# One fused adaLN / multi-query attention / SwiGLU block: from a generator that interleaves by budget to a list-scheduled task graph, with wider exps, denominators summed on VectorE and the MLP as filler

## The chip, the cores and the metric

The kernel runs on one core of one Trainium2 chip. The metric is the device time of one execution in microseconds (us). "Fast runs" are those of the undisturbed state; only these are compared. The engines are PE (TensorE, matrix multiply), ACT (ScalarE, exp and tanh), DVE (VectorE), POOL (GpSimd) and SP (issues DMA). The profile gives the share of the full TensorE clock that was granted; "warm" below means about 1.0, "cold" about 0.5. PV is the product of the exponentials with the values, and the *slot* of a group of matmuls is the time from its start on PE to the start of the next group.

## The reference

```python
# x: 2048 x 1024, 32 query heads of 32, ONE key and value head of 32, F = 3584
sa, ca, ga, sb, cb, gb = split(silu(c) @ w_mod)              # six modulation vectors of 1024
h = layernorm(x) * (1 + ca) + sa
q, k, v = h @ wq, h @ wk, h @ wv                             # k and v are shared by all heads
x = x + ga * (softmax(q k^T / sqrt(32)) v) @ wo
h = layernorm(x) * (1 + cb) + sb
x = x + gb * ((silu(h @ w1) * (h @ w3)) @ w2)
```

The work is cut into 4 blocks of 512 queries. A block has 8 "heads" (each a group of 4 query heads, packed into the 128 rows of the array), and a head has 16 key tiles of 128 keys. One key tile needs four score matmuls, 4 x 512 columns of exp, four PV matmuls and, in some form, the softmax denominators. There are 512 key tiles in all. The MLP of a block can only start when the attention of that block is done, so it runs as *filler* for PE beside the attention of the next block, and the MLP of the last block runs alone.

## The kernel before

All matmul filler comes from one queue of generators. After each key tile the queue is drained until a budget of 1700 ns is spent, in pieces of up to eight matmuls. The order of the instructions on PE is fixed by this, without regard to what waits for what.

```python
def exp_pair(kt, pair):                       # two exps of 1024 columns per key tile
    T.emit("act", lambda e: e.activation(U[:, uslot, g0:g0 + 2, :], S4[:, g0:g0 + 2, :], ACT.Exp, scale=SCALE), ...)
...
for kt in range(NKT):
    exp_pair(kt, 0)
    exp_pair(kt, 1)
    if kt + 1 < NKT:
        for g in range(4): s_mm(kt + 1, g)    # next scores, into the same four banks
    for g in range(4): pv(kt, g)              # PV sums, one bank
    for g in range(4): dd(kt, g)              # denominators: ones x U, another bank
    ...
    yield "B"                                 # -> drain(BUDGET)
...
BUDGET = 1700.0
MM512 = 216.0
CH = 8
def drain(budget):
    spent = 0.0
    while posts and spent < budget:
        spent += step(posts[0])               # one piece of filler, up to CH matmuls
```

PSUM has eight banks: four for scores, one for PV, one for denominators, two for all filler.

The softmax here doesn't subtract the row's maximum and nothing guards it: scores larger than these inputs give would overflow.

## Time and profile before

| | before |
|---|---|
| median of 4 runs | 1787.5 us (1779.3 to 1788.8) |
| first exp | 126.6 us |
| end of block 0 | 460.8 us |
| blocks 1, 2, 3 | 369.3, 367.1, 371.7 us |
| from there to the end | 209.8 us |

The block ends are read from the timeline: each head ends with one copy of the PV sums out of PSUM, and the eighth copy of a block is its end.

The head of the profile page of the kernel before; each figure is busy time and share of the span, the digits are tenths in 40 equal slices, PEclk the granted clock.

```profile
PE 1525.3 (86%) x9792; PEld 478.9 (27%) x9920; DVE 542.7 (31%) x844; ACT 1111.0 (62%) x1248; POOL 45.5 (3%) x76
...
PE   2476899989979999888899999887999988968997
...
ACT  2913578888667775687677755886677657821100
...
PEclk7687995555779999955899999557899997568999
```

No engine is full throughout. The clock row shows the pattern: it falls to 5 in four places, and these are the places where ACT is at 7 to 8 and the filler has run out.

Stretches of the kernel before: the stretch, its length, busy us (instructions) of PE, PE weight loads, DVE, ACT and POOL, then granted clock, DMA share and GB/s.

```profile
1249.00:1493.00 244.00, 226.03 (x1609) 78.88 (x1640) 83.23 (x139) 163.69 (x183) 0.00 (x0) 0.98 0.36 87
1493.00:1563.00 70.00, 63.50 (x394) 11.09 (x386) 10.54 (x6) 60.99 (x66) 0.00 (x0) 0.52 0.13 32
1600.00:1778.00 178.00, 157.85 (x722) 67.81 (x734) 65.53 (x137) 16.72 (x28) 0.00 (x0) 0.96 0.49 119
```

The first is block 3 with filler: PE is 93% busy at full clock and ACT 67%. In the second the filler is used up: ACT 87%, clock 0.52. The third is the MLP of the last block: PE is 89% busy and no other engine more than 37%.

The timeline of one filled key tile in the kernel before (start, length, engine, line, operation, output and inputs, count, idle time before):

```profile
557.12 0.40 PE L675 MATMUL S<-QT,KT 32*128 32x512 bf16 x4
...
557.45 0.40 PE L699 MATMUL AD<-HT,V 128*32 128x512 bf16 x4
...
557.58 1.94 ACT L689 ACTIVATE HT<-S 128x1024 bf16<-128x1024 f32 x2 [0.63 <-PE S L675]
557.67 0.39 PE L708 MATMUL AD<-HT,ONES 128*32 128x512 bf16 x4
557.99 1.90 PE L845 MATMUL PB<-HT,W1S 128*128 128x512 bf16 x8
...
559.83 0.40 PE L675 MATMUL S<-QT,KT 32*128 32x512 bf16 x4
```

Read the starts, not the lengths (ends of matmuls are modelled): scores 0.33, PV 0.22, denominators 0.32, eight filler matmuls 1.84, together 2.71 us, in which ACT works 1.94. ACT waits for PE.

The costliest groups before (line, engine, operation, shapes, count | busy us, mean ns | idle before):

```profile
L689 ACT ACTIVATE HT<-S 128x1024 bf16<-128x1024 f32 x1024 | 979.3, 1023 | 302.0 <-PE S L675 301.8
L675 PE MATMUL S<-QT,KT 32*128 32x512 bf16 x2048 | 353.8, 477 | 88.4 <-ACT HT L689 87.9
L708 PE MATMUL AD<-HT,ONES 128*32 128x512 bf16 x2048 | 261.7, 490 | 0.0
```

### The profile page before, as it was taken

The page shows a single profiled execution, that of the slowest core. Times are in us where ns is not written, and L with a number is a line of the kernel's source. Part 1 is how long each engine was busy: PE and PEld are TensorE (multiplying, and loading weights), DVE is VectorE, ACT ScalarE, POOL GpSimd, SP SyncE. Part 2 cuts the span into 40 slices and gives each one's busy share as a digit, 9 for nine tenths or more (in the row PEclk, how much of TensorE's full clock was granted, in tenths as well). Part 3 has the DMA queues.
Part 4 walks back from the last instruction along what each step waited for, and adds up shares of the span by engine and source line. Part 5 has one row for each costly group of instructions (what it writes and reads, how often), then busy time and mean ns, then how long its engine had stood idle before and what let it go on. Part 6 is the DMA issues. An engine that isn't in the chain of part 4 may idle for free.

```text
span 1778.8 us, 23745 instructions
## 1 busy us (share of the span) xinstructions
PE 1525.3 (86%) x9792; PEld 478.9 (27%) x9920; DVE 542.7 (31%) x844; ACT 1111.0 (62%) x1248; POOL 45.5 (3%) x76
## 2 busy tenths in 40 slices
PE   2476899989979999888899999887999988968997
PEld 0231321111223333311233333112333332123433
DVE  0530331121254441221543422114344321144431
ACT  2913578888667775687677755886677657821100
POOL 2300400000000000000000000000000000000000
PEclk7687995555779999955899999557899997568999
DMA  8104100000003343310033524200233443003465
GB/s 292 33 33 154 37 1 1 1 1 1 1 25 95 96 113 71 82 44 1 12 91 97 127 52 76 71 1 1 72 95 95 87 84 91 1 0 95 142 131 106
DMA packets 249373, 115.97 MB, mean 65 GB/s; under 512 B 119472, under 2 KB 242352, under 8 KB 249264
## 3 DMA queue, kind: packets, MB, share of 16 engines
q1 hardware_dynamic: 247344, 107.10, 24.0%
q0 software_dynamic: 1920, 7.34, 1.2%
q8 instruction: 78, 1.28, 0.3%
q14 instruction: 31, 0.25, 0.1%
HBM read 110.23 MB, written 4.19 MB: 64 GB/s over the span
## 4 chain that ended last, share of the span: by engine, by line
PE 74%; ACT 11%; DVE 9%; issue 4%; DMA 2%; POOL 0%; DVEq 0%; ACTq 0%; POOLq 0%; SPq 0%
PE S L675 13%; PE AD L699 12%; PE PB L861 11%; PE PB L845 11%; PE PB L850 10%; ACT HT L689 8%; PE AD L708 6%; PE PB L768 4%; PE PB L644 3%; DVE ADSB L738 2%; DVE O2B L867 1%; PE PB L477 1%; DVE ST L516 1%; ACT HT L596 1%; DVE ADSB L736 1%
## 5 line engine op out<-in xcount | busy, mean ns | idle before, releaser
L689 ACT ACTIVATE HT<-S 128x1024 bf16<-128x1024 f32 x1024 | 979.3, 1023 | 302.0 <-PE S L675 301.8
L675 PE MATMUL S<-QT,KT 32*128 32x512 bf16 x2048 | 353.8, 477 | 88.4 <-ACT HT L689 87.9
L699 PE MATMUL AD<-HT,V 128*32 128x512 bf16 x2048 | 261.1, 486 | 1.3 <-ACT HT L689 1.2
L708 PE MATMUL AD<-HT,ONES 128*32 128x512 bf16 x2048 | 261.7, 490 | 0.0
L845 PE MATMUL PB<-HT,W1S 128*128 128x512 bf16 x861 | 210.3, 385 | 27.2 <-DVE TT L831 16.3
L850 PE MATMUL PB<-HT,W3S 128*128 128x512 bf16 x865 | 207.5, 380 | 3.9 <-DVE TS L829 1.9
L861 PE MATMUL PB<-HHT,W2S 128*128 128x512 bf16 x861 | 206.5, 380 | 3.9 <-issue 2.3
L675 PEld LDWEIGHTS S<-QT,KT 32*128 32x128 bf16 x2048 | 75.1, 94 | 468.1 <-ACT HT L689 425.0
L827 ACT ACTIVATE TS<-PB 128x512 bf16<-128x512 f32 x112 | 66.9, 597 | 184.9 <-PE PB L845 184.9
L736 DVE COPY ADSB<-AD 128x1024 f32<-128x1024 f32 x32 | 39.1, 1221 | 389.4 <-PE AD L708 389.4
L845 PEld LDWEIGHTS PB<-HT,W1S 128*128 128x128 bf16 x896 | 80.1, 99 | 150.4 <-issue 40.6
L850 PEld LDWEIGHTS PB<-HT,W3S 128*128 128x128 bf16 x896 | 81.4, 98 | 120.4 <-issue 33.4
L861 PEld LDWEIGHTS PB<-HHT,W2S 128*128 128x128 bf16 x896 | 80.5, 98 | 113.7 <-issue 31.7
L738 DVE RECIPROCAL ADSB<-ADSB 128x512 f32<-128x512 f32 x32 | 107.3, 3353 | 1.1
L829 DVE TENSOR_SCALAR TS<-TS 128x512 bf16<-128x512 bf16 x112 | 32.8, 293 | 233.6 <-ACT TS L827 233.6
L699 PEld LDWEIGHTS AD<-HT,V 128*32 128x32 bf16 x2048 | 56.0, 96 | 177.8 <-issue 152.9
L833 DVE TENSOR_TENSOR HHT<-TT,PB 128x512 bf16<-128x512 bf16 x112 | 76.9, 687 | 88.1 <-PE PB L850 85.1
L867 DVE TENSOR_SCALAR O2B<-PB,GBT 128x512 bf16<-128x512 f32 x32 | 24.0, 751 | 223.9 <-PE PB L861 223.9
L831 DVE TENSOR_TENSOR TT<-TS,PB 128x512 bf16<-128x512 bf16 x112 | 77.1, 688 | 3.8
L768 PE MATMUL PB<-WO,ATT 128*128 128x512 bf16 x245 | 63.9, 412 | 11.9 <-DVE ATT L740 10.9
L708 PEld LDWEIGHTS AD<-HT,ONES 128*32 128x32 bf16 x2048 | 57.7, 103 | 0.0
L644 PE MATMUL PB<-HT,HHT 128*128 128x512 bf16 x216 | 52.7, 388 | 2.9 <-DVE QT L652 1.4
(84 smaller groups left out, 520.1 us busy)
## 6 DMA issues: line engine op xcount, KB each, us to landing
W1S<-in_B_w_dram SPq DMA_DIRECT2D x56, 512.0 KB, 3.9
W3S<-in_B_w_dram SPq DMA_DIRECT2D x56, 512.0 KB, 4.3
W2S<-in_B_w_dram SPq DMA_DIRECT2D x32, 896.0 KB, 6.0
X<-in_A_x_dram SPq DMA_DIRECT2D x4, 1024.0 KB, 13.2
W1S<-in_w_mod_dram SPq DMA_DIRECT2D x4, 1024.0 KB, 5.1
W3S<-in_w_mod_dram SPq DMA_DIRECT2D x4, 1024.0 KB, 5.1
out_dram<-X SPq DMA_DIRECT2D x4, 1024.0 KB, 5.4
W1S<-in_w_mod_dram POOLq DMA_DIRECT2D x3, 1024.0 KB, 10.1
```

Of the source, the lines that this page charges most:

```text
L644: fns = [lambda e, cc=cc, f=f, ap=ap: e.matmul(ap, WQ[:, cc, f * P:(f + 1) * P], HT[:, cc, qb * 512:(qb + 1) * 512], start=(cc == 0), stop ...
L675: T.emit("pe", lambda e, kt=kt, g=g: e.matmul(S4[:, g, :], KT[32 * g:32 * (g + 1), kt * P:(kt + 1) * P], QT[32 * g:32 * (g + 1), f, qb * 5 ...
L689: T.emit("act", lambda e, uslot=uslot, g0=g0: e.activation(U[:, uslot, g0:g0 + 2, :], S4[:, g0:g0 + 2, :], ACT.Exp, scale=SCALE), reads=[( ...
L699: T.emit("pe", lambda e, kt=kt, g=g, uslot=uslot, first=first, last=last: e.matmul(APS[32 * g:32 * (g + 1), :], V[:, kt, :], U[:, uslot, g ...
L708: T.emit("pe", lambda e, kt=kt, g=g, uslot=uslot, first=first, last=last: e.matmul(DPS[32 * g:32 * (g + 1), :], ONES[:], U[:, uslot, g, :] ...
L738: T.emit("dve", lambda e: e.reciprocal(ADSB[:, 1, :], ADSB[:, 1, :]), reads=["ADSB1"], writes=["ADSB1"])
L768: fns = [lambda e, f=f, tti=tti, fb=fb, pbk=pbk: e.matmul(PB[pbk][:, :], ATT[:, f, tti * P:(tti + 1) * P], WO[:, f, fb * 512:(fb + 1) * 51 ...
L831: T.emit("dve", lambda e, gs=gs: e.tensor_tensor(TT1[:, gs, :], TS[:, gs, :], PB0[:, :], ALU.mult), reads=[("TS", gs), ("PB", 0)], writes= ...
L833: T.emit("dve", lambda e, gs=gs, ft=ft: e.tensor_tensor(HHT[:, ft, :], TT1[:, gs, :], PB1[:, :], ALU.mult), reads=[("TT1", gs), ("PB", 1)] ...
L845: fns = [lambda e, cc=cc, slot=slot, sub=sub, H2T=H2T: e.matmul(PB0[:, :], W1S[:, slot, cc, sub * P:(sub + 1) * P], H2T[:, cc, :], start=( ...
L850: fns = [lambda e, cc=cc, slot=slot, sub=sub, H2T=H2T: e.matmul(PB1[:, :], W3S[:, slot, cc, sub * P:(sub + 1) * P], H2T[:, cc, :], start=( ...
L861: fns = [lambda e, fc=fc, slot=slot: e.matmul(PB0[:, :], W2S[:, slot, fc, :], HHT[:, fc, :], start=(fc == 0), stop=(fc == NF - 1)) for fc ...
```

## The change

The intent: describe all instructions as a graph of tasks with assumed durations, simulate the engines, and emit each engine's instructions in the order in which the simulation started them. Scores go first, then PV, then denominators, then filler, one matmul at a time, and a filler group gets a PSUM bank only when the simulation has one free. With it come a new cut of the exps, denominators that are mostly summed on VectorE, attention that starts as soon as the first 512 keys exist, and layernorms without passes for shift and scale. The core of the diff (almost every line of the file changes):

```diff
+            pick = min((c for c in cands if c[0] <= t + (slack if c[1].prio <= 1 else 0.001)), key=key)
+                    if n.cls == "S": r = 0                       # scores first
+                    elif n.cls == "V": ...  r = 1 or 4           # PV
+                    elif n.cls == "D": r = 2                     # denominators
+                    else: r = 3                                  # filler
...
-    S4 = psb("S4", [P, 4, 512], F32)
-    AD = psb("AD", [P, 2, 512], F32)
+    S5 = nc.alloc_psum_tensor("S5", [P, 5, 512], F32)            # banks 0-2, and 3 or 4 in turn
+    A = nc.alloc_psum_tensor("A", [P, 512], F32)
...
-    U[:, uslot, g0:g0 + 2, :], S4[:, g0:g0 + 2, :], ACT.Exp      # twice per key tile
+    U[:, u, 0:3, :], S5[:, 0:3, :], ACT.Exp                      # 1536 columns
+    U[:, u, 3, :], S5[:, s1, :], ACT.Exp                         # 512 columns, s1 = 3 + i % 2
...
-    DPS[32 * g:32 * (g + 1), :], ONES[:], U[:, uslot, g, :]      # for every key tile
+    TR[:, tr, :], TR[:, tr, :], U[:, u]..., ALU.add              # three adds of 2048 columns per four key tiles
+    PB[g.bank][...], ONES[:], TR[:, tr, ...]                     # ones-matmuls on the four sums of a head
...
+    # layernorm: (1 + scale) and shift applied per partition while the transposes leave PSUM
+    dst(c), PBH[g.bank][...], MODC[:, fm, c:c + 1], MODC[:, fs, c:c + 1], ALU.mult, ALU.add
...
+    g = grp()                                                    # filler: one task per matmul
+    for i0 in range(0, n, per): ...                              # per = 1
```

## The prediction

> **What bounds the kernel now.** No single engine does. The page gives PE 86%, ACT 62%, DVE 31% busy; the stretch table splits the 1778.8 us. Head: the first exps come at 126.6 us, then one pair per 6.8 us until 181, behind modulation blocks. Filled attention (516-756, 882-1127, 1249-1493): granted clock 0.98-1.00, PE about 93% busy, ACT about 67%. In the timeline one key tile takes 2.70 us there: scores 0.33, PV 0.22, denominators 0.32, eight MLP matmuls 1.83; two exps cover 1.94, so ACT waits for PE. Unfilled attention (210-463, 756-830, 1127-1197, 1493-1563): clock 0.50-0.60 and 2.09 us a key tile (4.18 for two); PE has no MLP work left. The Trainium skill, "TensorE: Matmul & The Clock Gate", Part 1, says that an array that is not busy enough runs at half clock; this trace agrees (0.50 against 1.00). Tail: last exp at 1567.8, then 211 us of WO, layernorm and MLP, PE-bound.
> So blocks alternate between too much filler and none.
>
> **What changes.**
> - Denominators: 2048 matmuls (262 us of PE busy) become 512; about 0.25 us a key tile leaves PE. VectorE gains 384 adds of 128x2048 bf16. A 128x1024 bf16 add takes 692 ns now; I estimate 1.22 us each, 470 us in all, so DVE goes from 543 to about 950 us busy.
> - Exps: 1024 at 1023 ns become 512 of 1536 columns plus 512 of 512. From 1023 (1024 columns) and 597 (512 columns) I estimate 1450 + 597: no ACT gain. The gain meant is that the next scores fit under the small exp. But banks 0-2 stay single: exp 1.45, then release plus scores plus visibility, about 0.1 + 0.46 us warm (score start 557.12, exp start 557.58) or 0.1 + 0.68 cold (321.78 to 322.46). That is a chain of about 2.0 us warm, 2.2 cold, a key tile.
> - Head: modulation as columns, the shift and scale folded into the transposes' evacuation, attention started per 512 keys: first exp near 45 us.
> - MLP spread matmul by matmul over the blocks; two PSUM banks for all filler.
> - Scale and shift passes of both layernorms (692 ns each), sqrt and its table loads go.
>
> **The sum.** PE per key tile warm: scores 0.33, PV 0.27, denominators 0.06, switches 0.1; filler of a block (672 MLP + 64 WO matmuls at about 0.22, transposes) about 165 us / 128 = 1.29. Together 2.05, level with the 2.0 us chain, so neither hides the other: I take 2.2-2.3.
> Head 45; block 0 (little filler, cold clock, layernorms of three blocks inside) 310; blocks 1-3, 290 each, 870; tail 205. Sum 1430 us. Nearly all PE saving is on the critical path; the rest comes from head and filler balance.
>
> **Right or wrong shows in:** first exp before 60 us; exps spaced about 2.2 us in all blocks, ACT busy 75% or more; clock near 1.0 in blocks 1-3, near 0.5-0.6 in block 0; denominator matmuls near 65 us; DVE 60-70% busy; last exp near 1225 us, then a tail near 200.
>
> **What would make it wrong.** DVE in order at about 80% in blocks 1-3: PSUM evacuations queued behind 1.2 us adds would stall filler, thus scores (slower, up to 1520). A static order built from assumed durations could stall PE's queue. Half clock in filled blocks would cost 200 us. Better interleaving could bring 1340.
>
> Predicted 1430 us, 1350 to 1520; faster 0.97, within 2% 0.02, slower 0.01.

## The result, and the profile after

| | before | after |
|---|---|---|
| median | 1787.5 us | 1398.9 us (1398.3 to 1400.4, 4 runs) |
| first exp | 126.6 us | 31.7 us |
| end of block 0 | 460.8 us | 338.4 us |
| blocks 1, 2, 3 | 369.3, 367.1, 371.7 us | 287.6, 287.7, 286.2 us |
| from there to the end | 209.8 us | 196.5 us |

The ratio is 0.7845 (95% interval 0.7823 to 0.7867). All ratios here are the mean time of one kernel's fast runs over that of the other's of the same rounds, so not quite the ratio of the medians. Of the 382 us between the two spans, 122 lie in the head and block 0, 247 in blocks 1 to 3 and 13 in the tail.

The head of the page after:

```profile
PE 1209.6 (87%) x8689; PEld 424.9 (30%) x8689; DVE 939.8 (67%) x1174; ACT 1046.8 (75%) x1142; POOL 17.3 (1%) x34
...
PE   4498985555899999988899999978999999789997
...
ACT  2378998888889999888899998989999989311100
...
PEclk9597995555899999998999999979999999889999
```

Apart from slice 2, in the head, the clock now has one hole, in slices 7 to 10, where before it had four.

Stretches after (columns as before):

```profile
200.00:338.00 138.00, 72.26 (x552) 12.36 (x544) 76.89 (x75) 119.91 (x125) 0.00 (x0) 0.53 0.12 29
414.00:560.00 146.00, 145.53 (x1047) 49.55 (x1046) 110.14 (x129) 133.80 (x153) 0.00 (x0) 1.00 0.37 100
883.00:913.00 30.00, 25.34 (x199) 8.27 (x197) 20.62 (x24) 28.29 (x31) 0.00 (x0) 0.96 0.57 125
```

These are three regimes of one loop. In the first there is no filler: PE is half idle and cold, and a head takes 36.1 us. In the second PE is busy 145.5 of 146 us, and a head takes 36.6 us. In the third, the last head of a block, PE is warm and nearly but not quite full, and a head takes 30.6 us. The same head time of 36 us has two opposite causes in the first two.

The timeline after, in a filled stretch:

```profile
453.12 0.40 PE L606 MATMUL S<-QT,KT 32*128 32x512 bf16 x4
...
453.45 1.25 PE L703 MATMUL PB<-QT,WREG 128*128 128x512 bf16 x5
453.56 1.45 ACT L613 ACTIVATE UREG<-S 128x1536 bf16<-128x1536 f32 x1
...
454.54 0.81 PE L711 MATMUL PB<-QT,WREG 128*128 128x512 bf16 x3
454.91 0.59 ACT L706 ACTIVATE HREG<-PB 128x512 bf16<-128x512 f32 x1
...
455.28 0.40 PE L606 MATMUL S<-QT,KT 32*128 32x512 bf16 x4
455.39 0.60 ACT L615 ACTIVATE UREG<-S 128x512 bf16<-128x512 f32 x1
```

Eight filler matmuls and one score group now fit into 2.16 us. (PV is done for two key tiles at once: its eight matmuls follow in the next key tile, which takes 2.27 us with six of filler.) The next scores no longer wait for the second exp: they start at 455.28, before the 512-column exp at 455.39.

The timeline after, in the cold stretch:

```profile
283.02 0.59 ACT L615 ACTIVATE UREG<-S 128x512 bf16<-128x512 f32 x1
283.18 0.61 PE L606 MATMUL S<-QT,KT 32*128 32x512 bf16 x4 [1.56 <-ACT UREG L613]
...
283.84 1.45 ACT L613 ACTIVATE UREG<-S 128x1536 bf16<-128x1536 f32 x1 [0.23 <-PE S L606]
```

PE had been idle for 1.56 us and could start the scores only when the wide exp had released banks 0 to 2. The next wide exp starts 0.66 us after the scores, and that is 0.23 us later than ACT could have taken it. This is a chain, not a full engine.

The groups that answer to those of before:

```profile
L613 ACT ACTIVATE UREG<-S 128x1536 bf16<-128x1536 f32 x512 | 744.1, 1453 | 150.7 <-PE S L606 140.1
L646 DVE TENSOR_TENSOR UREG<-UREG 128x2048 bf16<-128x2048 bf16 x256 | 310.9, 1214 | 82.8 <-ACT UREG L615 82.4
L606 PE MATMUL S<-QT,KT 32*128 32x512 bf16 x2048 | 222.5, 425 | 121.5 <-ACT UREG L613 118.3
L615 ACT ACTIVATE UREG<-S 128x512 bf16<-128x512 f32 x512 | 305.7, 597 | 0.0
...
L658 PE MATMUL PB<-UREG,ONES 128*32 128x512 bf16 x512 | 41.0, 449 | 1.7 <-DVE UREG L646 1.7
```

The exps cost what they cost before: 1453 + 597 ns against 2 x 1023. Per column this is (1453 - 597) / 1024 = 0.84 ns, which agrees with the 1.2 GHz that the Trainium skill gives in "ScalarE: Activation LUTs", Specifications. The adds take 1214 ns; the Trainium skill, "VectorE: DVE Perf Modes", "The perf-mode tier table", has 1224 ns for a bf16 add of 2048 elements, and this trace agrees. The denominator matmuls fall from 261.7 to 41.0 us busy.

### The profile page after: what moved, and what is told of

It is laid out like the page before. It is cut to its first block, busy times and chain, and to the rows that moved or that the text cites. A ratio compares the mean times of both kernels' runs of the same rounds, so it can differ in the third digit from the quotient of the medians.

```text
span 1396.4 us, 21161 instructions
## 1 busy us (share of the span) xinstructions
PE 1209.6 (87%) x8689; PEld 424.9 (30%) x8689; DVE 939.8 (67%) x1174; ACT 1046.8 (75%) x1142; POOL 17.3 (1%) x34
## 4 chain that ended last, share of the span: by engine, by line
PE 77%; ACT 11%; DVE 7%; issue 3%; POOL 1%; DMA 0%; SPq 0%; DVEq 0%; POOLq 0%; ACTq 0%
PE PB L703 15%; PE PB L711 15%; PE PB L722 14%; PE S L606 13%; ACT UREG L613 9%; PE A L624 7%; PE PB L682 4%; PE PB L506 4%; PE PB L658 3%; DVE ST L421 2%; DVE UREG L646 2%; ACT UREG L615 1%; DVE XN L438 1%; PE PB L452 1%; PE PB L490 1%
## 5 line engine op out<-in xcount | busy, mean ns | idle before, releaser
L613 ACT ACTIVATE UREG<-S 128x1536 bf16<-128x1536 f32 x512 | 744.1, 1453 | 150.7 <-PE S L606 140.1
L646 DVE TENSOR_TENSOR UREG<-UREG 128x2048 bf16<-128x2048 bf16 x256 | 310.9, 1214 | 82.8 <-ACT UREG L615 82.4
L606 PE MATMUL S<-QT,KT 32*128 32x512 bf16 x2048 | 222.5, 425 | 121.5 <-ACT UREG L613 118.3
L615 ACT ACTIVATE UREG<-S 128x512 bf16<-128x512 f32 x512 | 305.7, 597 | 0.0
L703 PE MATMUL PB<-QT,WREG 128*128 128x512 bf16 x896 | 226.6, 386 | 1.3 <-DVE QT L467 1.3
L640 DVE TENSOR_TENSOR UREG<-UREG 128x2048 bf16<-128x2048 bf16 x128 | 155.6, 1215 | 106.3 <-ACT UREG L615 105.7
L711 PE MATMUL PB<-QT,WREG 128*128 128x512 bf16 x896 | 222.6, 381 | 0.0
L722 PE MATMUL PB<-HREG,WREG 128*128 128x512 bf16 x896 | 214.3, 380 | 0.0
L624 PE MATMUL A<-UREG,V 128*32 128x512 bf16 x2048 | 178.3, 429 | 6.5 <-ACT UREG L615 5.6
L667 DVE RECIPROCAL DSB<-DSB 128x128 f32<-128x128 f32 x128 | 116.7, 932 | 0.9
L703 PEld LDWEIGHTS PB<-QT,WREG 128*128 128x128 bf16 x896 | 80.1, 98 | 118.8 <-issue 43.0
L711 PEld LDWEIGHTS PB<-QT,WREG 128*128 128x128 bf16 x896 | 81.0, 98 | 111.9 <-issue 29.0
L722 PEld LDWEIGHTS PB<-HREG,WREG 128*128 128x128 bf16 x896 | 79.2, 98 | 108.0 <-issue 30.3
L506 PE MATMUL PB<-HREG,WREG 128*128 128x512 bf16 x256 | 63.9, 385 | 0.1
```

What stands on the lines that cost most here:

```text
L506: g = mm_group(NC, lambda e, b, c: e.matmul(b[:], WQ[:, c, f * P:(f + 1) * P], HT[:, c, sl], start=c == 0, stop=c == NC - 1), lambda c: [( ...
L606: r = e.matmul(S5[:, b, j * qn:(j + 1) * qn], KT[32 * gg:32 * gg + 32, kt * P:(kt + 1) * P], QT[32 * gg:32 * gg + 32, f, q0:q0 + qn], star ...
L613: G.add("act", lambda e, u=u: e.activation(U[:, u, 0:3, :], S5[:, 0:3, :], ACT.Exp, scale=SCALE), reads=["S3"], writes=[("U", u, 0)] + uk, ...
L615: G.add("act", lambda e, u=u, s1=s1: e.activation(U[:, u, 3, :], S5[:, s1, :], ACT.Exp, scale=SCALE), reads=[("S1", s1)], writes=[("U", u, ...
L624: r = e.matmul(A[32 * gg:32 * gg + 32, 0:qn], V[:, kt, :], U[:, pu, gg, j * qn:(j + 1) * qn], start=kt == 0, stop=kt == NT - 1, tile_posit ...
L640: G.add("dve", lambda e, tr=tr, u=u, fu=first_u: e.tensor_tensor(TR[:, tr, :], U[:, fu].rearrange("p g s -> p (g s)"), U[:, u].rearrange(" ...
```

## The experiments

The theory after the result: in blocks 1 to 3 PE is full and its work sets the time; in block 0 the chain exp, scores, exp sets it, lengthened by the cold clock; and the gain comes from less PE work, an earlier start and filler that is spread well. The rivals: VectorE's in-order queue sets the pace of the filler; the cut of the exps is the main source; the spread alone is.

### half_adds: is VectorE the bound?

```diff
-  TR[:, tr, :], TR[:, tr, :], U[:, u]..., ALU.add
+  TR[:, tr, 0:1024], TR[:, tr, 0:1024], U[:, u]...[:, 0:1024], ALU.add     # and the ones-matmuls read only these columns
```

> The changed kernel with each of the 384 adds cut to 1024 of its 2048 columns (wrong denominators on purpose), static order unchanged. VectorE falls from 940 to about 730 us busy. Theory (PE and the score-exp chain bound): within 1%, 1385 to 1400 us. Rival (VectorE's queue bounds the filled blocks): faster by 40 us or more, filled heads from 36.6 to 34 us or less.

Measured: 1386.0 us (ratio 0.7766 against 0.7845 for the full change; the result is wrong). Taking some 200 us off VectorE's 940 gave 1%. The stretch from 414 to 560 us in this kernel:

```profile
414.00:560.00 146.00, 144.90 (x1036) 49.41 (x1034) 86.20 (x130) 134.26 (x152) 0.00 (x0) 1.00 0.36 98
```

VectorE fell from 110 to 86 us there, and PE stayed full with the same number of matmuls. The filled heads stay at 36.6 us. VectorE is not the bound of the filled blocks. The 13 us are gained in small pieces: 4 us in block 0 and 1 to 3 us in each of the first two heads of blocks 1 and 2, where layernorm work stands in VectorE's queue.

### exp1024 and den_on_pe, and both again

These undo the cut of the exps, and on top of it the sums on VectorE.

```diff
 # exp1024: two score groups of two matmuls, two exps of 1024 columns, four banks
+ for hf in range(2):
+     scores of heads 2*hf, 2*hf+1 -> S5[:, 2*hf:2*hf+2, :]
+     exp U[:, u, 2*hf:2*hf+2, :] <- S5[:, 2*hf:2*hf+2, :], prio=0
 # den_on_pe: as exp1024, and ones x U for every key tile into the free bank S5[:, 4, :]; no adds
 # exp1024_b, den_on_pe_b: the same two, the second exp with prio=hf (0, then 1)
```

> The changed kernel with the exps cut as before: two of 1024 columns, and the scores as two groups of two matmuls, four banks. Theory (filled blocks are PE-bound, the exp cut gives ACT nothing): filled heads stay at 36.6 us for 16 key tiles or gain up to 1.6 us from one more switch of PE per key tile; the cold heads of block 0 fall from 36.1 towards 31 us, because the next scores of one pair run under the exp of the other. Total 1375 to 1440 us. Rival (the wide exp with its five banks is a main source of the gain): 1460 us or more, blocks 1 to 3 over 300 us each.

> exp1024 and, in the bank that it leaves free, the denominators back on PE as 2048 matmuls, with no adds on VectorE. To be read against exp1024. Theory (PE-bound in filled blocks): about 0.2 us more a key tile there, 2.6 to 3.5 us a head, so plus 50 to 90 us in all; DVE falls to about 470 us busy without any help. Rival (VectorE's queue of adds holds up PSUM evacuation and so sets the pace): equal to exp1024 or faster.

Measured: exp1024 1758.2 us (ratio 0.983; its profile is of a slow run), den_on_pe 1588.9 us (0.891). Both expectations of the theory were missed: exp1024 is 25% over the change, and adding PE work made it faster. The edit had an unmeant part. In the change the second exp has the priority of the MLP's tanh, in these two it had the higher one, so the order put the tanh behind exps; it was taken that filler groups then kept their banks, and that filler slid behind the last exp for that reason. So both were run again with that one number mended.

> exp1024 again with its second exp at the priority that the second exp has in the changed kernel, so that the MLP's tanh is no longer put behind every exp in the static order (in exp1024 the tanh waited 411 us for matmuls that waited for banks, and half the MLP slid behind the last exp). Theory (sum of PE's work): two score groups of two matmuls hold the array as long as one of four each, about 0.3 us more PE a key tile, 5 us a head; total 1450 to 1560 us, with ACT no busier. Rival (the first result was only the starved tanh): within 2% of the changed kernel, 1370 to 1425 us.

> den_on_pe with the same mended priority; to be read against exp1024_b. Theory (sum of PE's work): 1536 more ones-matmuls, four at a time, at 0.054 us each: 60 to 100 us more than exp1024_b, with DVE half idle. Rival (the adds on VectorE cost as much in stalls as they save): within 25 us of exp1024_b, or faster.

Measured: exp1024_b 1560.1 us (0.872; fast runs 1547.8 to 1566.4, its profile again of a slow run), den_on_pe_b 1568.1 us (0.875; its profile is of a fast run). The first is at the edge of what the theory expected; one number in the priorities was worth about 200 us in exp1024, but only 21 us in den_on_pe. By its size the rival of exp1024 was right: with the priority mended, undoing the cut of the exps still costs some 160 us (149 to 168 by the fast runs), more than any other sound edit here. The second expectation was missed: putting the denominators back cost nothing measurable here, not 60 to 100 us. So this pair does not show what the sums on VectorE are worth.

Nor did the mended priority bring the filler back. ACT in the page of den_on_pe_b, 40 slices of 39 us:

```profile
ACT  2497999765799999999999999999500111001100
```

From slice 12 to 28 the exps run nearly without a pause, blocks 1 to 3 take 289, 249 and 255 us (286 to 288 in the change), and the work after the last head takes 451 us in place of 196: 1814 matmuls with weights start after the last exp, where the change has 736, the WO and MLP of one block. The time that this run loses against the change is all behind the last exp. What PE does more is in its groups:

```profile
L607 PE MATMUL S<-QT,KT 32*128 32x512 bf16 x2048 | 414.9, 411 | 26.3 <-ACT UREG L613 23.4
...
L629 PE MATMUL S<-UREG,ONES 128*32 128x512 bf16 x2048 | 170.8, 413 | 0.0
```

The same 2048 score matmuls keep PE busy 414.9 us in groups of two and 222.5 in groups of four. The timeline of den_on_pe_b says why:

```profile
600.99 0.39 PE L607 MATMUL S<-QT,KT 32*128 32x512 bf16 x2
601.31 0.60 PE L679 MATMUL PB<-QT,WREG 128*128 128x512 bf16 x2
601.84 0.39 PE L607 MATMUL S<-QT,KT 32*128 32x512 bf16 x2
```

Two score matmuls take a slot of 0.32 us, as four did (0.33, above; the medians are 0.320 for 416 groups of two from 450 to 860 us, and after the change 0.327 for 180 groups of four from 414 to 560 and 626 to 914 us), since the members of a group run side by side in different rows of the array. This is what the Trainium skill tells in "TensorE: Matmul & The Clock Gate", Part 3, of packed matmuls (the span of a pack is nearly that of one). So the change's cut 3 + 1, released together, saves a slot per key tile over 2 + 2, some 512 x 0.32 = 164 us of PE as an estimate from these slots. It gives ACT nothing. The estimate is close to what exp1024_b lost, but PE's gaps and clock moved too, so that is no proof. One thing more moved along: the simulation took 0.24 us for a score group of either size, so the order of these runs counts less PE work than there was.

And the clock can be cold while PE is full. Two stretches of den_on_pe_b:

```profile
350.00:400.00 50.00, 50.00 (x218) 9.94 (x221) 13.38 (x22) 29.96 (x30) 0.00 (x0) 0.50 0.00 0
600.00:650.00 50.00, 50.00 (x384) 14.42 (x387) 17.39 (x24) 49.62 (x57) 0.00 (x0) 1.00 0.16 46
```

PE shows 50.00 of 50 busy in both; in the first it issues 218 matmuls at clock 0.50, in the second 384 at 1.00. PE has no gap at all in the first, so this is not a queue that ran dry. Since exp1024_b has no fast profile, whether such stretches explain why it is no faster than den_on_pe_b stays open.

### before_even: is it the spread alone?

```diff
-    BUDGET = 1700.0
+    BUDGET = 1290.0
-    CH = 8
+    CH = 2
```

> The kernel before with two constants changed: MLP filler in pieces of 2 matmuls and 6 per key tile where it had 8. Nothing else moves, PE work is the same. Theory (the spread of the filler is a large part of the gain): a filled key tile takes 0.87 + 6 x 0.216 + 0.1 = 2.27 us where it took 2.70, and few key tiles are left without filler at half clock; blocks 1 to 3 fall from 369 to 300-320 us each, total 1570 to 1680 us. Rival (PE work saved is what counts): within 2% of 1787 us.

Measured: 1719.7 us (0.964). The direction is right and the size is not: blocks 1 to 3 fall from 369 to about 350 us, not to 300-320. The timeline of this kernel in a filled head:

```profile
600.06 0.69 DVE L831 TENSOR_TENSOR TT<-TS,PB 128x512 bf16<-128x512 bf16 x1
...
600.80 2.20 PE L845 MATMUL PB<-HT,W1S 128*128 128x512 bf16 x6 [1.70 <-DVE TT L831]
...
603.61 1.94 ACT L689 ACTIVATE HT<-S 128x1024 bf16<-128x1024 f32 x2 [3.65 <-PE S L675]
```

PE stands 1.70 us before a filler group, because its PSUM bank is still being read, and the scores behind it stand too, so ACT idles 3.65 us. A fixed quota puts a matmul into the queue without knowing whether its bank is free. After the change no such wait is seen from 414 to 560 us: PE is full, with the same two banks.

But such waits are not the reason for the missed size. PE waits for that VectorE instruction (L831) before a filler group six times in blocks 1 to 3, 8.9 us in all (12 and 16.0 us in the kernel before). The even quota did what it was meant to do with the clock, whose mean in these blocks rises from 0.86 to 0.94 (0.96 after the change). What it still takes more than the change, 1049 against 862 us for the three blocks, is mostly PE's own time: 949 us busy against 809. So about 140 of these 188 us are PE work, slots included. This is read from modelled busy times and not from an edit, but it speaks for the saving of PE work more clearly than the pair above.

### bunch8: one matmul at a time

```diff
-    def mm_group(n, f, reads_f, n_cols=512, per=1, prio=5, late=0):
+    def mm_group(n, f, reads_f, n_cols=512, per=8, prio=5, late=0):
```

> The changed kernel with the filler emitted in pieces of eight matmuls, as before, in place of single ones. Theory: PE's sum of work is the same, but scores wait up to 1.8 us behind a piece, so a filled key tile takes about 2.4 to 2.7 us and fewer of them, the rest runs unfilled at half clock, like the kernel before: 1430 to 1500 us. Rival (only the sum of PE's work counts): within 1.5% of the changed kernel.

Measured: 1515.7 us (0.850), 117 us slower than the change and a little more than expected. Timeline:

```profile
500.91 1.90 PE L711 MATMUL PB<-QT,WREG 128*128 128x512 bf16 x8
501.96 0.61 ACT L615 ACTIVATE UREG<-S 128x512 bf16<-128x512 f32 x1
502.74 0.39 PE L606 MATMUL S<-QT,KT 32*128 32x512 bf16 x4
...
503.19 1.45 ACT L613 ACTIVATE UREG<-S 128x1536 bf16<-128x1536 f32 x1 [0.62 <-PE S L606]
```

The wide exp ended near 502.1 (it starts at 500.63 and takes 1.45), the scores start at 502.74 behind the piece of eight, and ACT waits. Filled heads take about 43 us, the unfilled ones at the ends of blocks 36. The same scheduler with coarse pieces loses 30% of its gain (117 of 389 us).

### late_start: what the early start is worth

```diff
+  late = [("KT", i) for i in range(4)] + qkeys(NC - 1, q0, qn) if q0 == 0 and f == 0 else []   # first scores wait for these
```

> The changed kernel with the first scores made to wait for the keys of all four blocks and for the last query head of block 0, so that no exp runs beside the first layernorms and projections. Theory (block 0 is bound by exps and their chain after the head, so the early exps of the first 100 us are time gained): first exp about 100 to 110 us, 30 to 50 us slower: 1430 to 1450 us. Rival (PE's or VectorE's work in the head sets the end of block 0 anyway): within 1%.

Measured: 1434.5 us (0.804), 36 us slower, as expected, though the first exp came at 85.3 us and not at 100. The early exps are about 36 us of the 122 that the head and block 0 gained.

### front256 and tail256: smaller blocks at one end

```diff
-    BLOCKS = [(i * 512, 512) for i in range(NTB)]
+    BLOCKS = [(0, 256), (256, 256), (512, 512), (1024, 512), (1536, 512)]       # front256
+    BLOCKS = [(0, 512), (512, 512), (1024, 512), (1536, 256), (1792, 256)]      # tail256
```

> The changed kernel with its first block of 512 query columns cut into two of 256, nothing else. Theory (the time is the sum of PE's work, and PE's one large gap is the stretch of block 0 from 200 to 338 us, 53% busy at half clock, because no MLP work exists yet): the first MLP work now comes at about 130 us and fills that stretch; it costs one more sweep over the MLP weights with 256 columns, some 20 us of PE. Net 30 to 80 us faster, 1315 to 1370 us, clock near 1.0 from 150 us on. Rival (the 196 us tail without exps is the gap that counts, or DVE and the exps set the pace): 1395 us or more.

> The changed kernel with its last block of 512 query columns cut into two of 256, nothing else. The tail after the last exp falls from 196 to about 105 us. Theory (sum of PE's work): the work taken out of the tail lands in stretches where PE is already full, so nothing is gained, and the extra sweep over the weights costs: 1390 to 1430 us, last exp 80 us or more later. Rival (the tail without exps is time lost): 60 us or more faster, below 1340 us.

Measured: front256 1396.9 us (0.782, no different from the change), tail256 1436.5 us (0.805). The gain of 30 to 80 us that was expected of the first did not come. Stretches of front256:

```profile
200.00:338.00 138.00, 121.83 (x1834) 74.70 (x1834) 92.60 (x152) 129.97 (x158) 2.00 (x3) 0.96 0.53 140
540.00:620.00 80.00, 42.24 (x324) 7.37 (x326) 43.40 (x42) 69.59 (x73) 0.00 (x0) 0.53 0.08 22
```

The hole of block 0 was filled, as meant, and came back from 540 to 620 us. The likely fault of the reasoning: up to the end of the first 1024 queries the filler on offer is the query projections and the MLP of the first 512, however these are cut. Filling a gap earlier only uses it up earlier.

tail256 was expected to be slower, and was, but not as described. The last exp stayed where it was (the last head ends at 1200.7 us, after the change 1199.9), and the work behind it took 231 us in place of the 105 expected:

```profile
1202.00:1433.00 231.00, 186.42 (x1498) 140.05 (x1497) 80.01 (x188) 21.45 (x56) 2.27 (x6) 0.94 0.77 186
```

The MLP work did not find room among the attention of the short blocks and ran behind it, after all: 1408 weight matmuls of 256 columns start after the last exp, nearly as much work as the 736 of 512 columns after the change. Both fit "PE's work has to go somewhere"; neither gives a gain.

### warm3 and warm_paced: the cold clock by itself

```diff
 # warm3
+ if q0 == 0 and f in (4, 5, 6, 7):
+     mm_group(3, lambda e, b, c: e.matmul(b[:], IDENT[:], KT[:, 0:512], ...), ...)
 # warm_paced
+ if q0 == 0 and f >= 4:
+     mm_group(4, lambda e, b, c, u=u: e.matmul(b[:], IDENT[:], U[:, u, 0, :], ...), lambda c, u=u: ["IDENT", ("U", u, 0), ("UR", u)])
```

> The changed kernel with three dummy matmuls (identity times keys, 512 columns, result never read) per key tile in heads 4 to 7 of block 0, where the granted clock was 0.50 to 0.61 and PE 53% busy; results stay right. Theory (those heads are bound by the chain exp of 1536, scores, exp of 1536, whose scores run at half clock): clock near 1.0 there, heads from 36.1 to 31-32 us, 15 to 22 us faster in all: 1375 to 1386 us. Rival (these heads are bound by ACT or VectorE, or dummies only take PE time): 1395 us or more, heads of 36 us or longer.

Measured: 1397.0 us (0.783), no gain: missed. The dummies depended on nothing but the keys, so the scheduler took them all at once. Stretches of warm3:

```profile
200.00:266.00 66.00, 63.73 (x464) 21.45 (x462) 38.61 (x39) 59.51 (x62) 0.00 (x0) 1.00 0.26 60
266.00:338.00 72.00, 38.06 (x292) 6.62 (x288) 39.47 (x39) 61.99 (x65) 0.00 (x0) 0.53 0.00 1
```

The first half is warm and full, the second cold as before.

> The changed kernel with four dummy matmuls per key tile in heads 4 to 7 of block 0, this time tied to that tile's exp (identity times the exps just written), so that the static order can't pull them forward as it did in warm3, where they ran from 200 to 266 us and heads 6 and 7 stayed at clock 0.52 and 36.1 us. Results stay right. Theory (those heads are bound by the chain exp, scores, exp, whose scores run at half clock when PE has no filler): clock above 0.9 from 200 to 338 us, heads 4 to 7 at 31-32 us in place of 36.1, block 0 over at 318-323 us, the rest unchanged: 1376 to 1385 us. Rival (ACT or VectorE sets those heads, or the clock is not PE's to keep): heads of 35 us or more, within 0.5% of the changed kernel.

Measured: 1385.2 us (1384.4 to 1386.3, 5 fast runs; ratio 0.7762, interval 0.7736 to 0.7787), results correct. This is the fastest correct kernel of the study. The same stretch:

```profile
200.00:322.00 122.00, 101.48 (x775) 29.83 (x792) 74.22 (x72) 118.40 (x124) 0.00 (x0) 1.00 0.13 29
```

ACT is now busy 118 of 122 us. Heads 5 to 7 of block 0 take 32.1 us each in place of 36.1, and block 0 ends at 322.0 us in place of 338.4; 13 of these 16 us remain at the end. PE does *more* work than without the dummies and the kernel is faster, because the work that matters runs at full clock. The chain theory of block 0 stands: the edit changes no instruction of ACT or VectorE.

## Why the prediction was right

The prediction was 1430 us in a range of 1350 to 1520; measured were 1398.9. All three terms of its sum came out 1 to 5% too long, so no error hid another. Term by term:

- *Head 45 and block 0 310*, together 355: measured 338.4. The first exp came at 31.7 us, not 45. The half clock was foreseen, and measured at 0.53 from 200 to 338 us; warm_paced shows that it costs those heads 4 us each. Part of block 0 was warm (1.00 from 150 to 200 us), which the prediction's "near 0.5-0.6 in block 0" did not see.
- *Blocks 1 to 3, 290 each*: measured 287.6, 287.7, 286.2. The pace taken, 2.2 to 2.3 us a key tile, is the mean that was measured (287.2 / 128 = 2.24), but "neither hides the other" is right only of the mean, and that is in part luck. The prediction spread 736 filler matmuls evenly, 5.75 a key tile, and came to 2.05 us of PE beside a chain of 2.0. The order puts 7 on each key tile of the filled heads; with 1.25 more at 0.22 the prediction's own sum is 2.3, and PE alone, full, gives the measured 2.29 (36.6 us a head). In the last head of a block only 3.8 are left, and it takes 30.6 us, 1.91 a key tile, near the chain. The two bounds take turns by head; they don't add up within a key tile.
- *Tail 205*: measured 196.5.
- *No ACT gain from the exps*: 1453 + 597 ns, as estimated. What the new cut gives was named only in part. The prediction saw that the scores fit under the small exp; exp1024_b (some 160 us slower) and the slots of den_on_pe_b say that releasing four scores in one slot, where 2 + 2 takes two, is the larger point.
- *DVE about 950 us busy, at 80% no bound*: 939.8, 75% of blocks 1 to 3, and half_adds shows that it isn't the bound.
- *Denominators near 65 us*: 41.0. The estimate was a quarter of 262, but that 262 contained many half-clock matmuls (166 ns busy each from 756 to 830 us, 98 from 516 to 756).
- *"Nearly all PE saving is on the critical path"*: not shown by an edit. PE is full in the filled heads, so by the slots (PV and denominators from 0.54 to about 0.34 us a key tile) the sums on VectorE should be worth some 3 us in each of them, but the one pair of runs meant to show it (exp1024_b against den_on_pe_b) moved by 0.3% only, with other things moving as well. The busy times of before_even and the change speak for it (140 of 188 us in blocks 1 to 3).
- *Head and filler balance for the rest*: shown in part. The early start is worth 36 us (late_start), the single-matmul granularity 117 (bunch8), an even quota without knowledge of the banks only 62 (before_even against its own baseline median of 1781.5).

These parts are not additive: each was taken from the whole alone, and what is left then meets another bound.

## What to carry to other kernels

A filler matmul belongs in PE's queue only where the latency-critical matmul behind it can bear the wait: emitting filler one matmul at a time and not in eights was worth 117 us here. What it is worth to know when a PSUM bank is free was not tested alone; in before_even the waits of that kind are 9 us in three blocks. Group small packed matmuls: two scores cost PE the same 0.32 us as four. Before blaming an engine for a slow stretch, look at the granted clock beside its busy share: the same head time stood for a full PE in one stretch and for a cold, half idle PE in another, and cheap dummy matmuls, tied to the pace of the loop, were a cure for the second (13 us). When a static order comes from priorities, treat each priority as part of the experiment: one number moved a run by 200 us, and look afterwards whether the mended number did what it was mended for; here the filler stayed behind.

## What the Trainium skill lacked or had wrong

- "TensorE: Matmul & The Clock Gate", Part 1 and "Loop structure matters more than you think", explains a half clock by idle gaps of PE, long ones or frequent short ones. It lacks a full queue that stays at half clock (a caveat of Part 1 tells only of a clock stuck at a quarter): den_on_pe_b from 350 to 400 us shows PE busy 50.00 of 50 us at clock 0.50. (PE busy is modelled, and "Trainium Kernel Development and Optimization", Performance Expectations, warns that matmul busy time is a bad metric for the distance from the roofline; this is a case of it.) How much array work keeps the clock up is on none of its pages; four 512-column dummies per key tile did (1.00, longest gap of PE 0.59 us), none did not (0.53, longest gap 1.56 us).
- The same page, Part 3, gives the span of a pack by itself. It lacks the slot of a small pack in a mixed stream: 0.32 to 0.33 us for a score group, of two or of four alike, between other matmuls, where full matmuls of 512 columns in a row start every 0.22 us (27 such steps take 5.83 us in the tail of the change).
- "VectorE: DVE Perf Modes" has no row for the reciprocal in its tier table. Here 128x512 in fp32 took 3353 ns before, and 128x128 took 932 ns after, so 6.3 ns for each further element of a partition.
